# VectorE's exp banks chosen while scores are ordered, other spare banks in the first block, and PV of the last units ahead of other work

**The chip, the cores and the metric.** One core of one Trainium2 chip. The metric is the device time of one execution. It is the span of the trace plus about 1.83 us.

## The reference, cut to what matters

```python
xn = _layernorm(x)                          # x: 1 x 2048 x 448, bf16
s = _A_ref(xn, A_wqkv, A_wo)                # 16 heads of 28: softmax(q k^T / sqrt(28)) v, then @ wo
g = _silu(_B_ref(xn, w1, b1, w2, b2))       # gelu MLP, 448 -> 1792 -> 448
return x + s * g
```

The exponential (exp) of 16 x 2048 x 2048 scores is the main work. PV below is the product of these probabilities with v, on TensorE (PE).

## The kernel before

The program is written by a scheduler on the host. Processes yield tasks with a modelled duration; the scheduler always takes the task with the earliest modelled start, and appends it to the list of its engine. On the chip each engine has its list and waits on semaphores; that PE keeps to the order of its list shows below, in a stand of 1.65 us with the next scores queued behind it. The modelled durations therefore fix the order.

```python
def start_of(self, t):                      # the model's earliest start of a task
    s = self.tE[t.E]
    for b in t.reads:
        ...
        s = max(s, b.tw + SEM)              # SEM = 0.07 us after the modelled write
    ...
```

A block is one group of four heads by 512 queries: 64 score banks (128x512 f32 each). Block 0 works in units of two banks, the others in units of three; a ring of six banks holds two units. The third bank of some units (from a table, `LATE`) is exponentiated by VectorE with a polynomial, in pairs; ScalarE exponentiates the rest.

```python
COUNTS = (5, 4, 5, 4, 5, 5, 5, 6, 1, 6, 6, 6, 6, 4)     # VectorE's banks per block 1..14
...
    _b0 = 2 * (_i % 2) if _i < 32 else 3 * (_i % 2)     # first ring bank of a unit
...
K.banks += [(K.ring[:, b, :], K.b_ring[b]) for b in (5, 4)]   # block 0's spares
```

`p_busy` adds filler matmuls where the model sees PE under 85% busy; they are meant to keep PE's clock up. (In the first trace of before the granted clock was 1.00 from 7.57 to 475.20 us and 0.50 after, and PE had been busy 1.98 of the 3.41 us before the fall.)

## Time and profile before

| | before |
|---|---|
| time, median of 3 | 487.23 us |
| span of the traced run (its time was 488.98 us) | 487.2 us |
| first exp starts | 13.50 us |
| first exp to the end of the last | 464.84 us |
| after the last exp | 8.83 us |
| ScalarE / VectorE / PE busy | 96% / 84% / 93% |

The lines of the profile are in the prediction.

### The profile page before, as it was taken

What the parts mean: (1) busy time and instruction counts of PE and PEld (TensorE: products, weight loads), DVE (VectorE), ACT (ScalarE), POOL (GpSimd) and SP (SyncE); (2) the same over time, 40 slices, a digit from 0 to 9 for tenths busy, and PEclk for the clock granted to TensorE, in tenths of its full rate; (3) what the DMA queues carried; (4) which work ended last, traced back from release to release, by engine and by line L of the source; (5) the groups of instructions that cost most, each with busy time, mean ns of one, the idle gap of its engine ahead of it and who ended that gap; (6) DMA issues with size and microseconds to landing.
All of it is one profiled execution on the core that took longest, in us unless ns stands there. A gap on an engine that the chain in (4) does not pass through costs nothing.

```text
span 487.2 us, 9867 instructions
## 1 busy us (share of the span) xinstructions
PE 451.6 (93%) x4107; PEld 174.2 (36%) x4107; DVE 407.6 (84%) x566; ACT 469.5 (96%) x391; POOL 85.4 (18%) x91
## 2 busy tenths in 40 slices
PE   6999999999999999999999999999999999999875
PEld 4443333333233333232333343333233443343432
DVE  8745998779996998998999499899898989999553
ACT  4999999999999999999999999999999999999992
POOL 6472112031021113020111041110200202020100
PEclk9999999999999999999999999999999999999995
DMA  8401000000000000000400000000100010001210
GB/s 251 142 12 25 1 0 1 1 1 1 2 1 1 0 1 1 1 2 1 133 1 0 1 1 1 1 2 1 38 1 2 1 39 0 1 20 60 90 44 20
DMA packets 8286, 11.07 MB, mean 23 GB/s; under 512 B 1649, under 2 KB 6897, under 8 KB 8242
## 3 DMA queue, kind: packets, MB, share of 16 engines
q1 hardware_dynamic: 8098, 10.21, 6.9%
q8 instruction: 32, 0.52, 0.4%
q10 hardware_dynamic: 144, 0.23, 0.1%
q14 instruction: 12, 0.10, 0.1%
HBM read 8.61 MB, written 1.84 MB: 21 GB/s over the span
## 4 chain that ended last, share of the span: by engine, by line
ACT 43%; PE 29%; issue 17%; DVE 9%; POOL 1%; ACTq 0%; DVEq 0%
ACT P L1115 38%; PE ring L1086 8%; PE acc L1234 5%; PE misc L1034 4%; ACT h L1013 3%; PE misc L692 2%; PE acc L823 2%; PE misc L976 2%; DVE x_sb L1142 1%; PE misc L1323 1%; PE acc L805 1%; DVE x_sb L1193 1%; DVE kT L1187 1%; PE ring L976 1%; POOL rlo L1299 1%
## 5 line engine op out<-in xcount | busy, mean ns | idle before, releaser
L1115 ACT ACTIVATE P<-ring 128x1536 bf16<-128x1536 f32 (+1 forms) x350 | 428.8, 1461 | 2.6 <-PE ring L1086 2.0
L1086 PE MATMUL ring<-qT,kT 32*128 32x512 bf16 (+1 forms) x1208 | 136.3, 350 | 20.7 <-ACT P L1115 16.4
L1234 PE MATMUL acc<-P,vaug 128*32 128x512 bf16 (+1 forms) x1140 | 96.2, 354 | 0.1
L1086 PEld LDWEIGHTS ring<-qT,kT 32*128 32x128 bf16 x1208 | 36.7, 91 | 125.9 <-ACT P L1115 113.2
L1298 POOL CAST rhi<-rc 128x512 bf16<-128x512 f32 x15 | 18.1, 1206 | 228.5 <-DVE rc L1294 185.5
L1142 DVE TENSOR_SCALAR x_sb<-ring 128x512 int32<-128x512 f32 x68 | 46.7, 686 | 9.4 <-PE ring L1086 8.6
L1034 PE MATMUL misc<-w,h 128*128 128x448 bf16 x224 | 52.3, 355 | 0.0
L823 PE MATMUL acc<-ident,zero 128*128 128x128 bf16 x588 | 49.9, 221 | 0.0
L1234 PEld LDWEIGHTS acc<-P,vaug 128*32 128x32 bf16 x1140 | 26.0, 95 | 53.7 <-issue 48.0
L899 POOL TENSOR_TENSOR qsq<-qT 128x512 bf16<-128x512 bf16 x15 | 21.8, 1454 | 129.6 <-DVE qT L894 123.2
L823 PEld LDWEIGHTS acc<-ident,zero 128*128 128x128 bf16 x588 | 33.7, 98 | 22.5 <-issue 21.1
L976 PE MATMUL misc<-xnT,w 128*128 128x512 bf16 x140 | 38.5, 382 | 0.1
L1193 DVE SCALAR_TENSOR_TENSOR x_sb<-x_sb,kT 128x1024 uint16<-128x1024 int32 (+1 forms) x22 | 28.2, 1280 | 0.3
L1191 DVE SCALAR_TENSOR_TENSOR kT<-kT 128x1024 f32<-128x1024 f32 (+1 forms) x22 | 27.6, 1252 | 0.3
L959 DVE CAST h<-misc 128x512 bf16<-128x512 f32 x35 | 24.0, 687 | 4.4 <-PE misc L976 3.8
L1187 DVE SCALAR_TENSOR_TENSOR kT<-kT 128x1024 f32<-128x1024 f32 (+1 forms) x22 | 27.2, 1238 | 0.4
L1189 DVE SCALAR_TENSOR_TENSOR kT<-kT 128x1024 f32<-128x1024 f32 (+1 forms) x22 | 26.5, 1203 | 0.3
L1034 PEld LDWEIGHTS misc<-w,h 128*128 128x128 bf16 x224 | 17.3, 97 | 22.7 <-issue 11.8
L1299 POOL TENSOR_TENSOR rlo<-rc,rhi 128x512 bf16<-128x512 f32 x15 | 22.3, 1489 | 1.2
L1187 DVE SCALAR_TENSOR_TENSOR w<-w 128x1024 f32<-128x1024 f32 (+1 forms) x19 | 21.8, 1149 | 0.3
L1193 DVE SCALAR_TENSOR_TENSOR x_sb<-x_sb,w 128x1024 uint16<-128x1024 int32 (+1 forms) x19 | 21.2, 1114 | 0.1
L1189 DVE SCALAR_TENSOR_TENSOR w<-w 128x1024 f32<-128x1024 f32 (+1 forms) x19 | 20.8, 1094 | 0.2
(144 smaller groups left out, 479.2 us busy)
## 6 DMA issues: line engine op xcount, KB each, us to landing
h<-in_A_x_dram SPq DMA_DIRECT2D x4, 448.0 KB, 3.5
w<-in_B_w_dram SPq DMA_DIRECT2D x1, 1568.0 KB, 7.2
x_sb<-in_A_x_dram SPq DMA_DIRECT2D x3, 448.0 KB, 6.0
w<-in_B_w_dram SPq DMA_DIRECT2D x1, 1344.0 KB, 8.2
out_dram<-h SPq DMA_DIRECT2D x6, 224.0 KB, 2.4
h<-in_A_wqkv_dram SPq DMA_DIRECT2D x3, 168.0 KB, 5.5
out_dram<-h SPq DMA_DIRECT2D x4, 112.0 KB, 1.7
wo<-in_A_wo_dram SPq DMA_DIRECT2D x16, 24.5 KB
```

Source lines behind the costliest of these rows:

```text
L823: ins = eng.matmul(K.acc[:, 0:128], K.zero[:, :], K.ident[:, :], start=False, stop=True, skip_group_check=True)
L976: ins = eng.matmul(bank, K.w1[:, kt, ft * 128:(ft + 1) * 128], K.xnT[:, kt, c * 512:(c + 1) * 512], start=(kt == 0), stop=(kt == KT - 1))
L1034: ins = eng.matmul(ps, hv[:, ft, t * 128:(t + 1) * 128], K.w2[:, ft, :], start=(ft == 0), stop=(ft == FT - 1))
L1086: return eng.matmul(K.ring[:, RB[m], col:col + nq], K.kT[32 * j:32 * j + 32, g, t * 128:(t + 1) * 128], K.qT[32 * j:32 * j + 32, g, c * 51 ...
L1115: return eng.activation(K.P[:, p0:p0 + n, :], K.ring[:, b0:b0 + n, :], ACTF.Exp, scale=SM_SCALE)
L1142: yield _Task(DVE, lambda eng, m=m, i=i, half=half: eng.tensor_scalar(K.ysb[i][:, 512 * half:512 * half + 512], K.ring[:, RB[m], :], SM_SC ...
L1187: yield _Task(DVE, lambda eng: eng.scalar_tensor_tensor(u, v, EXP_A, v, op0=ALU.add, op1=ALU.mult), [tv], [tu], d1, 0.0, 4)
L1189: yield _Task(DVE, lambda eng: eng.scalar_tensor_tensor(u, u, EXP_B, u, op0=ALU.add, op1=ALU.mult), [tu], [tu], d1, 0.0, 4)
L1191: yield _Task(DVE, lambda eng: eng.scalar_tensor_tensor(u, v, EXP_D, u, op0=ALU.mult, op1=ALU.add), [tv, tu], [tu], d1, 0.0, 4)
L1193: yield _Task(DVE, lambda eng: eng.scalar_tensor_tensor(pl.bitcast(dt.uint16), y, 2.0 ** -9, u, op0=ALU.mult, op1=ALU.add), ty + [tu], [K. ...
L1234: return eng.matmul(K.acc[32 * j:32 * j + 32, q0:q0 + nq], K.vaug[:, t, 4 * g + j, :], ap[:, col:col + nq], tile_position=(0, 32 * j), sta ...
L1299: yield _Task(En, lambda eng: eng.tensor_tensor(K.rlo[:, :, :], rcb, K.rhi[:, :, :], ALU.subtract), [K.b_rc, K.b_rhl], [K.b_rhl], d2, 0.0, 1)
```

## The change

The intent: let the scheduler give a bank to VectorE when VectorE's modelled backlog allows it, remove a wait where block 0's two-bank units meet the first three-bank unit, and shorten the end. The core of the diff (cut):

```diff
-LATE, PAIR = set(), {}
...
-COUNTS = (5, 4, 5, 4, 5, 5, 5, 6, 1, 6, 6, 6, 6, 4)
...
+    UBASE.append(4 * (_u % 2) if _u < 32 else 3 * (_u % 2))
...
+LATE_GAP, LATE_TH, LATE_SLACK, LATE_SUB = 3, 8.0, 6.0, 14
...
-        K.banks += [... for b in (5, 4)]
+        K.banks += [... for b in (3, 2)]
...
 def pe_low(self):
-        return ... < HAM_LOW * HAM_WIN
+        return ... < (HAM_LOW if K.exp_u < NU - 20 else 1.1) * HAM_WIN
 def p_busy(self):
-        while K.exp_u < NU - 1:
+        while K.exp_u < NU - 2:
...
 def p_silu(self, c):                       # VectorE's multiplies
-                        ... 0.63, 0.0, 6)
+                        ... 0.63, 0.0, 3)
 def p_scores(self):
+            K.assign(u)                    # chooses ScalarE's and VectorE's banks of unit u
-            ... + 0.02 * (len(fl) - len(ms))
+            ... + 0.005 * (len(fl) - len(ms))
+    def pick_late(self, u):
+        ...
+        left = (n - 1 - r) / 3.0 * 1.364 + LATE_SLACK
+        if K.open:
+            if u - K.open.u < LATE_GAP:
+                return False
+            if K.backlog() + 3.6 > left:
+                K.close()
+                return False
+            ...                            # the second bank of the open pair
+        else:
+            bl = K.backlog()
+            ...
+            if not K.ys or bl > LATE_TH or bl + 4.8 > left or sub > LATE_SUB:
+                return False
+            ...                            # opens a pair, takes one of two buffers
 def p_pv(self):
-                        lambda: 1.2 if K.exp_u - K.pv_u > 4 or GU - 1 <= K.exp_u <= GU else 6)
+                        lambda: 1.2 if K.exp_u - K.pv_u > 4 or K.exp_u > NU - 4 or GU - 1 <= K.exp_u <= GU else 6)
```

In `p_pv` the modelled duration of block 15's PV is shortened too; that edit is not shown, and below "the edit of `p_pv`" means the rank line alone.

More of the change, by code (lines that the diff above doesn't have):

```diff
@@ L29 @@
 MTOT = NBLK * T * 4
-LATE, PAIR = set(), {}
-OFFS = {0: (), 1: ((7,),), 2: ((0,), (7,)), 3: ((0, 3), (10,)), 4: ((0, 3), (7, 11)), 5: ((0, 3), (6, 9), (13,)),
-        6: ((0, 3), (6, 9), (11, 13)), 7: ((0, 2), (4, 7), (9, 11), (13,)), 8: ((0, 2), (4, 6), (8, 10), (12, 14)),
-        9: ((0, 1), (3, 5), (6, 8), (10, 12), (14,))}
-COUNTS = (5, 4, 5, 4, 5, 5, 5, 6, 1, 6, 6, 6, 6, 4)
 GM = 64 * 9 + 6
 MPAIRS = [tuple(64 * 9 + x for x in p) for p in ((16, 21), (26, 31), (36, 41), (46, 51))]
-for _ms in MPAIRS:
-    LATE.update(_ms)
-    for _m in _ms:
-        PAIR[_m] = _ms
@@ L42 @@
-MLATE = set(LATE)
-_seq = [m for m in range(64, MTOT) if m not in MLATE]
-_US = [list(range(m, m + 2)) for m in range(0, 64, 2)] + [_seq[i:i + UB] for i in range(0, len(_seq), UB)]
-GU = min(u for u, ms in enumerate(_US) if ms[-1] >= GM)
-for _b in range(1, NBLK - 1):
-    _th = [ms[2] for ms in _US if len(ms) == 3 and ms[2] // 64 == _b and ms[2] % 64 >= 4]
-    for _o in OFFS[COUNTS[_b - 1]]:
-        _ms = tuple(_th[x] for x in _o)
-        LATE.update(_ms)
-        for _k in _ms:
-            PAIR[_k] = _ms
@@ L54 @@
-UNITS, RB, PB, RPREV, PPREV, UOF = [], {}, {}, {}, {}, {}
-_last, _plast, _p = {}, {}, 0
-for _i, _ms in enumerate(_US):
-    _b0 = 2 * (_i % 2) if _i < 32 else 3 * (_i % 2)
-    _na = len([m for m in _ms if m not in LATE])
-    if _p + _na > NP:
-        _p = 0
-    UNITS.append((_ms, _ms[:_na], _b0, _p))
-    for _k, m in enumerate(_ms):
-        UOF[m] = len(UNITS) - 1
-        RB[m] = _b0 + _k
-        RPREV[m] = _last.get(RB[m])
-        _last[RB[m]] = m
-        if _k < _na:
-            PB[m] = _p + _k
-            PPREV[m] = _plast.get(PB[m])
-            _plast[PB[m]] = m
-    _p += _na
+MLATE = set(m for ms in MPAIRS for m in ms)
@@ new lines @@
+_seq = [m for m in range(64, MTOT) if m not in MLATE]
+UNITS = [list(range(m, m + 2)) for m in range(0, 64, 2)] + [_seq[i:i + UB] for i in range(0, len(_seq), UB)]
+GU = min(u for u, ms in enumerate(UNITS) if ms[-1] >= GM)
+RB, RPREV, UOF, UBASE, _last = {}, {}, {}, [], {}
+for _u, _ms in enumerate(UNITS):
+    UBASE.append(4 * (_u % 2) if _u < 32 else 3 * (_u % 2))
+    for _k, _m in enumerate(_ms):
+        UOF[_m] = _u
+        RB[_m] = UBASE[_u] + _k
+        RPREV[_m] = _last.get(RB[_m])
+        _last[RB[_m]] = _m
@@ L97, in __init__ @@
         self.tr = 0.0
+class _Pair:
+    __slots__ = ("i", "u", "ms", "done", "closed")
+    def __init__(self, i, u, m):
+        self.i, self.u, self.ms, self.done, self.closed = i, u, [m], 0, False
 class _Task:
@@ L414, in schedule @@
         K.pv_done = [False] * MTOT
-        K.late_left = [len([m for m in LATE if m // 64 == b]) for b in range(NBLK)]
+        K.late = set(MLATE)
+        K.late_left = [len([m for m in MLATE if K.sub_of(m) == b]) for b in range(NBLK + 3)]
+        K.late_q = deque()
+        K.late_on = False
+        K.open = None
+        K.dve_q = 0.0
+        K.PB, K.PPREV, K.plast, K.pptr = {}, {}, {}, 0
+        K.act_ms, K.p0 = [None] * NU, [0] * NU
         K.ys, K.pls, K.pl_use = [0, 1], [0, 1, 2], [0, 0, 0]
@@ L418, in schedule @@
         K.late_blk = 0
-        K.banks += [(K.ring[:, b, :], K.b_ring[b]) for b in (5, 4)]
+        K.banks += [(K.ring[:, b, :], K.b_ring[b]) for b in (3, 2)]
         K.outs = []
@@ L429, in schedule @@
         K.spawn(K.p_scores(), 0)
-        K.spawn(K.p_take(4), 0)
-        K.spawn(K.p_take(5), 0)
+        K.spawn(K.p_take(2), 0)
+        K.spawn(K.p_take(3), 0)
         K.spawn(K.p_exps(), 0)
@@ L757, in tr @@
         def tr(pr, h):
-            bank, tok = ring(2 * h + pr)
+            bank, tok = ring(4 * h + pr)
             psb = bank.bitcast(dt.bfloat16)
@@ L771, in trev @@
             for h in range(2):
-                bank, tok = ring(2 * h + pr)
+                bank, tok = ring(4 * h + pr)
                 src = bank.bitcast(dt.bfloat16)[:, 0:512].rearrange("p (k n) -> p k n", k=2)
@@ L813, in pe_low @@
             K.pe_hist.popleft()
-        return sum(b - max(a, now - HAM_WIN) for a, b in K.pe_hist) < HAM_LOW * HAM_WIN
+        return sum(b - max(a, now - HAM_WIN) for a, b in K.pe_hist) < (HAM_LOW if K.exp_u < NU - 20 else 1.1) * HAM_WIN
     def p_busy(self):
@@ L825, in f @@
             return ins
-        while K.exp_u < NU - 1:
-            yield ("until", lambda: K.pe_low() or K.exp_u >= NU - 1)
+        n = 0
+        while K.exp_u < NU - 2:
+            yield ("until", lambda: K.pe_low() or K.exp_u >= NU - 2)
             yield _Task(PE, f, [K.b_id, K.b_pads], [K.b_acc], DUM, 0.1, 95)
+            n += 1
+            if n > 2000:
+                raise RuntimeError("stuck")
     def p_k0(self):
@@ L982, in p_direct @@
         K = self
-        s0 = UNITS[GU - 1][2]
+        s0 = UBASE[GU - 1]
         for i, (c, f0) in enumerate(DIRECT):
@@ L995, in p_gelu @@
         left = [FT] * C
-        s0 = UNITS[GU - 1][2]
+        s0 = UBASE[GU - 1]
         for q, pc in enumerate(PIECES):
@@ L1052, in p_silu @@
                                                                        op0=ALU.add, op1=ALU.mult),
-                        [K.b_sig[c % 2], K.b_fsb[c % 2]], [K.b_h[c], K.b_g[c]], 0.63, 0.0, 6)
+                        [K.b_sig[c % 2], K.b_fsb[c % 2]], [K.b_h[c], K.b_g[c]], 0.63, 0.0, 3)
         K.g_done[c] = True
@@ L1074, in p_scores @@
         for u in range(NU):
-            ms = UNITS[u][0]
+            ms = UNITS[u]
             fl, rd = [], []
@@ L1103, in p_scores @@
             yield ("until", lambda: all(RPREV[m] is None or K.ring_rel[RPREV[m]] for m in ms))
-            yield _Task(PE, fall, rd, [K.b_ring[RB[m]] for m in ms], 0.17 + 0.05 * len(ms) + 0.02 * (len(fl) - len(ms)), 0.1, 1)
+            K.assign(u)
+            yield _Task(PE, fall, rd, [K.b_ring[RB[m]] for m in ms], 0.17 + 0.05 * len(ms) + 0.005 * (len(fl) - len(ms)), 0.1, 1)
             K.sc_u = u
@@ L1109, in p_exps @@
         for u in range(NU):
-            _, ms, b0, p0 = UNITS[u]
+            yield ("until", lambda: K.sc_u >= u)
+            ms, b0, p0 = K.act_ms[u], UBASE[u], K.p0[u]
             n = len(ms)
-            yield ("until", lambda: K.sc_u >= u and all(PPREV[m] is None or K.pv_done[PPREV[m]] for m in ms))
+            yield ("until", lambda: all(K.PPREV[m] is None or K.pv_done[K.PPREV[m]] for m in ms))
             def fexp(eng, b0=b0, p0=p0, n=n):
@@ L1120, in p_exps @@
             K.exp_u = u
-            K.exp_m = UNITS[u + 1][0][0] - 1 if u + 1 < NU else MTOT - 1
+            K.exp_m = UNITS[u + 1][0] - 1 if u + 1 < NU else MTOT - 1
             if u >= NU - 2:
@@ L1131, in p_late @@
                 b.r += x.r
-        for u in range(NU):
-            for m in UNITS[u][0]:
-                if m not in LATE:
-                    continue
-                half = PAIR[m].index(m)
-                if half == 0:
-                    yield ("until", lambda: K.sc_u >= u and len(K.ys) > 0)
-                    i = K.ys.pop(0)
-                else:
-                    yield ("until", lambda: K.sc_u >= u)
-                yield _Task(DVE, lambda eng, m=m, i=i, half=half: eng.tensor_scalar(
-                    K.ysb[i][:, 512 * half:512 * half + 512], K.ring[:, RB[m], :], SM_SCALE * LOG2E * 65536.0,
-                    127.0 * 65536.0, op0=ALU.mult, op1=ALU.add),
-                            [K.b_ring[RB[m]]], [K.b_y[i][half]], 0.69, 0.0, 1)
-                K.ring_rel[m] = True
-                if m == PAIR[m][-1]:
-                    K.spawn(K.p_exp2(PAIR[m], i), m)
+        K.late_on = True
@@ new lines, in p_late @@
+        while K.sc_u < NU - 1 or K.late_q:
+            yield ("until", lambda: K.sc_u == NU - 1 or (K.late_q and UOF[K.late_q[0][0]] <= K.sc_u))
+            if not K.late_q:
+                return
+            m, i, half, pair = K.late_q.popleft()
+            yield _Task(DVE, lambda eng, m=m, i=i, half=half: eng.tensor_scalar(
+                K.ysb[i][:, 512 * half:512 * half + 512], K.ring[:, RB[m], :], SM_SCALE * LOG2E * 65536.0,
+                127.0 * 65536.0, op0=ALU.mult, op1=ALU.add),
+                        [K.b_ring[RB[m]]], [K.b_y[i][half]], 0.69, 0.0, 1)
+            K.dve_q -= 0.69
+            K.ring_rel[m] = True
+            pair.done += 1
+            if pair.closed and pair.done == len(pair.ms):
+                K.spawn(K.p_exp2(tuple(pair.ms), i), m)
@@ new lines, in backlog, with close @@
+    def backlog(self):
+        K = self
+        t = max(0.0, K.tE[DVE] - K.now) + K.dve_q
+        for p in K.procs:
+            if isinstance(p[3], _Task) and p[3].E == DVE and p[3].prio != 4 and p[3].prio != 1:
+                st = K.start_of(p[3])
+                if st is not None and st < K.now + 1.0:
+                    t += p[3].dur
+        return t
+    def close(self):
+        K = self
+        p, K.open = K.open, None
+        p.closed = True
+        if p.done == len(p.ms):
+            K.spawn(K.p_exp2(tuple(p.ms), p.i), p.ms[-1])
@@ new lines, in pick_late @@
+    def pick_late(self, u):
+        K = self
+        ms = UNITS[u]
+        m = ms[-1]
+        sub = K.sub_of(m)
+        if K.open and (u - K.open.u > LATE_GAP + 2 or K.sub_of(K.open.ms[0]) != sub):
+            K.close()
+        n = 64 if sub < NBLK - 1 else 16
+        r = m % n
+        if len(ms) < 3 or not K.late_on or sub == 0 or r < 4 or GU - 1 <= u <= GU + 1:
+            return False
[4 more added lines that the diff above has]
+            if K.backlog() + 3.6 > left:
+                K.close()
+                return False
+            p = K.open
+            p.ms.append(m)
+            K.late_q.append((m, p.i, 1, p))
+            K.close()
+        else:
+            bl = K.backlog()
+            one = max(bl, 4.1) + 7.2 > left
+            if not K.ys or bl > LATE_TH or bl + 4.8 > left or sub > LATE_SUB:
+                return False
+            p = _Pair(K.ys.pop(0), u, m)
+            K.late_q.append((m, p.i, 0, p))
+            K.open = p
+            if one:
+                K.close()
+        K.late.add(m)
+        K.late_left[sub] += 1
+        K.dve_q += 3.6
+        return True
@@ L1150, in p_mlate, with assign @@
+    def assign(self, u):
+        K = self
+        ms = UNITS[u][:-1] if K.pick_late(u) else UNITS[u]
+        if K.pptr + len(ms) > NP:
+            K.pptr = 0
+        for k, m in enumerate(ms):
+            K.PB[m] = K.pptr + k
+            K.PPREV[m] = K.plast.get(K.pptr + k)
+            K.plast[K.pptr + k] = m
+        K.act_ms[u], K.p0[u] = ms, K.pptr
+        K.pptr += len(ms)
     def p_mlate(self):
@@ L1155, in p_mlate @@
             i = K.ys.pop(0)
+            K.dve_q += 7.2
             for half, m in enumerate(ms):
@@ L1166, in p_mlate @@
                     127.0 * 65536.0, op0=ALU.mult, op1=ALU.add), [tok], [K.b_y[i][half]], 0.69, 0.0, 1)
+                K.dve_q -= 0.69
                 K.banks.append((bank, tok))
@@ L1195, in p_exp2 @@
                     ty + [tu], [K.b_pl[k]], d1, 0.0, 4)
+        K.dve_q -= 2.91 * len(ms)
         K.ln2e = 0
@@ L1209, in p_pv @@
             first, end = K.sub_of(ms[0]), K.pieces(ms[-1])[3]
-            b = q // 16
+            b = first
             yield ("until", lambda: K.exp_m >= ms[-1] and K.E_done >= first - 1 and (
-                not end or len([x for x in K.late_ready if x[0] // 64 == b]) == K.late_left[b]))
+                not end or len([x for x in K.late_ready if K.sub_of(x[0]) == b]) == K.late_left[b]))
             late = []
             for m, k, half in list(K.late_ready):
-                hole = (4 * q + m % 4) in LATE and all(m % 4 != x[0] % 4 for x in late)
-                if m // 64 == b and (end or (K.ready([K.b_pl[k]]) and (hole or len(K.late_ready) - len(late) > 3))):
+                hole = (4 * q + m % 4) in K.late and all(m % 4 != x[0] % 4 for x in late)
+                if K.sub_of(m) == b and (end or (K.ready([K.b_pl[k]]) and (hole or len(K.late_ready) - len(late) > 3))):
                     late.append((m, k, half))
@@ L1220, in p_pv @@
             K.late_left[b] -= len(late)
-            src = [(m, K.P[:, PB[m], :], K.b_P[PB[m]]) for m in ms if m not in LATE]
+            src = [(m, K.P[:, K.PB[m], :], K.b_P[K.PB[m]]) for m in ms if m not in K.late]
             src += [(m, K.plate[k][:, 512 * half:512 * half + 512], K.b_pl[k]) for m, k, half in late]
@@ L1227, in p_pv @@
                     _, j, pc, _, s = K.pieces(m)
-                    g = b // C
+                    g = q // 16 // C
                     if kk >= len(pc):
@@ L1244, in fall @@
                 return ins
-            yield _Task(PE, fall, rd, [K.b_acc], 0.36 if len(fl) < 5 else 0.6, 0.1,
-                        lambda: 1.2 if K.exp_u - K.pv_u > 4 or GU - 1 <= K.exp_u <= GU else 6)
+            yield _Task(PE, fall, rd, [K.b_acc], 0.36 if len(src) < 5 else 0.6, 0.1,
+                        lambda: 1.2 if K.exp_u - K.pv_u > 4 or K.exp_u > NU - 4 or GU - 1 <= K.exp_u <= GU else 6)
             for m in ms:
```

## The prediction

Passages that told of the hardware what no trace or run of this case shows are cut from the text below, and the cuts are marked. None of them is a term of its sum, which came to 482.5 us. The 0.1 to 0.2 us for a semaphore in part 3 compare with 0.15 us in tail_only's trace, from the end of the last exp (478.26) to the PV that waits for it (478.41).

> **What bounds the kernel now.** I read the page first (busy shares, slices), then the groups by form, the waits, the table of stretches, the end of the chain of waits, and the timeline of the switch out of block 0.
>
> ```profile
> PE 451.6 (93%) x4107; PEld 174.2 (36%) x4107; DVE 407.6 (84%) x566; ACT 469.5 (96%) x391; POOL 85.4 (18%) x91
> PEclk9999999999999999999999999999999999999995
> ...
> L1115 ACT ACTIVATE P<-ring 128x1536 bf16<-128x1536 f32 x249 | 350.6, 1602 | 1.2 <-PE ring L1086 0.9
> L1115 ACT ACTIVATE P<-ring 128x1024 bf16<-128x1024 f32 x100 | 108.9, 1119 | 1.4 <-PE ring L1086 1.1
> L1142 DVE TENSOR_SCALAR x_sb<-ring 128x512 int32<-128x512 f32 x68 | 46.7, 686 | 9.4 <-PE ring L1086 8.6
> ...
> ACT P L1115 <- PE ring L1086: 2.0, 4, 0.7
> ...
> 13.50:45.80 32.30, 31.33 (x285) 13.40 (x284) 17.63 (x37) 30.66 (x37) 15.93 (x20) 1.00 0.19 56
> 45.80:449.30 403.50, 383.41 (x3184) 141.22 (x3183) 360.39 (x456) 402.87 (x317) 57.89 (x41) 1.00 0.03 9
> 449.30:478.30 29.00, 23.80 (x530) 12.15 (x531) 14.85 (x30) 29.00 (x23) 2.20 (x2) 0.95 0.21 65
> 478.30:487.20 8.90, 3.81 (x54) 1.56 (x44) 3.39 (x7) 0.04 (x1) 0.00 (x0) 0.50 0.08 26
> ```
>
> In the last four lines the columns are PE, PEld, DVE, ACT, POOL, then the granted clock. The stretches are block 0, blocks 1 to 14, block 15 and the tail after the last exp. ScalarE is busy 402.87 of 403.50 us in blocks 1 to 14: exp on ScalarE is the bound there, and only exp taken off ScalarE shortens them. PE's 93% is no second bound: 588 of its matmuls are fillers (line 823, 49.9 us busy)[...]. Outside the exps there are three fixed pieces: 13.5 us before the first exp, 27 us of gelu in block 9, and 8.9 us after the last exp.
>
> The kernel computes 1024 score banks (128x512). VectorE makes 76 of the exponentials (68 here, 8 during gelu) with a five-instruction polynomial; ScalarE makes 948, in 350 instructions of mostly three banks. Read from the starts of the exp instructions, a three-bank exp follows its predecessor by 1.33 us and a two-bank one by 0.904 us, so a bank moved to VectorE saves ScalarE 1.33 - 0.904 = 0.426 us. (The mean durations 1602 and 1119 overlap their neighbours and must not be used for this.)
>
> The tail and the switch out of block 0:
>
> ```profile
> 477.60 0.48 PE misc L1323
> 478.08 0.97 PE acc L1234 x32
> 479.05 1.23 PE ring L1323 x3
> 480.29 0.55 PE acc L1234 x16
> 480.83 0.45 PE acc L823 x3
> ...
> 481.30 0.30 DVE E_sb L1266
> ...
> 44.92 0.33 PE L823 MATMUL acc<-ident,zero 128*128 128x128 bf16 x3
> 45.32 0.61 PE L1086 MATMUL ring<-qT,kT 32*128 32x512 bf16 x6
> 45.75 1.45 ACT L1115 ACTIVATE P<-ring 128x1536 bf16<-128x1536 f32 x1 [0.58 <-PE ring L1086]
> ```
>
> The last exp ends at 478.34. PE, at half clock since about 475.3 (granted 0.60 in 475 to 476, 0.50 after), does older PV (x32), then an output projection (line 1323, 1.23 us), then the PV that the end needs (x16), then a filler. Only at 481.30 can VectorE read the accumulator: 2.96 us after the last exp.
>
> [...]the trace's scalar-tensor-tensor groups have means of 1227 to 1314 ns. [...]Here the clock fell although PE was busy 1.08 of 2.00 us in 472 to 474[...]. [...]the four last output transfers land after a median 1.7 us, and this part does not change.
>
> **The change part by part.**
>
> 1. Choice of VectorE's banks. The fixed table (68 banks) goes; when a unit of scores is ordered, its third bank is given to VectorE if the modelled backlog is under 8 us, a buffer is free and the work fits before the block's end. Units stay as they are, so the exp count stays 350; each added bank turns a three-bank exp into a two-bank one. How many can VectorE take? A bank costs 0.686 (eviction) plus half a pair: about (0.78 + 4 x 1.26)/2 = 2.91, together 3.6 us. In blocks 1 to 14 VectorE is busy 360.4 us; less 76 x 3.6 = 274 leaves 87 us of other work. Its fullest blocks (3, 11, 12, 13) still show 1.9 to 2.3 us idle each, as short gaps between instructions; I take 1.9 of a 27 us block as unavoidable, about 28 us of the 403.5. Usable: 403.5 - 28 - 87 = 288 us, or 80 banks, against 76. By block, idle above 1.9 us is 4.0 in block 2, 2.4 in block 4, about 5 in block 9 (twice as long, so twice the allowance), 3 elsewhere: 14.6 us, also 4 banks. So the table was already near VectorE's limit. I expect 4 more, 72 for 68, with a spread of -2 to +8: 4 x 0.426 = 1.7 us, all of it on the path.
>
> 2. Spare banks in block 0. Before, block 0's pairs use ring banks 0,1 and 2,3 and the spares are 4,5; the first three-bank unit (0,1,2) must wait for the exp that reads 2,3. That is the last line above: 0.58 us idle, 0.75 us start to start (1.655 instead of 0.904). With pairs on 0,1 and 4,5 it finds bank 2 free. Gain 0.75 us; nothing else in block 0 changes its order of need.
>
> 3. PV of the last units first, and fillers. In the last 20 units fillers take every modelled PE hole, so the clock should not fall near 475. At full clock the second-last exp is not late: it starts 1.73 us before the last one instead of 1.33, so 0.4 us. PV of the last units outranks the output projection from the fourth-last unit on, so PE has nothing old to do when the last exp ends: semaphore 0.1 to 0.2, PV x16 0.41 (its duration at 461 to 468), and no filler behind it. The accumulator is read about 0.7 us after the last exp, not 2.96: 2.2 us less. Then the same ladder, 481.30 to 485.03, with one or two matmuls at full clock: 0.2 less. Against this: the projection that needs only three groups (x3, 0.74 at full clock) may still be placed just ahead of the last PV because it can start earlier, 0.4 back. Sum 0.4 + 2.2 + 0.2 - 0.4 = 2.4 us.
>
> 4. Silu's multiplies on VectorE go ahead of the polynomial, and modelled durations of block 15's scores and PV are shortened to what the trace has (0.40 us per 12 score matmuls). ScalarE waits for nothing in block 15 until its last unit, so 0 us; I allow 0.2 us of loss for more two-bank units, whose short exps leave PE less time for the next scores.
>
> Sum: 487.2 - 1.7 - 0.75 - 2.4 + 0.2 = 482.5 us.
>
> **The rivals.** (a) VectorE is the real limit, and the dynamic choice yields no more banks, or fewer, since it also refuses near block ends and makes some lone banks (0.686 + 3.17 = 3.85 us). For: fullest blocks at 91 to 93%. Against: blocks 2, 4 and 9 have room. Then only parts 2 and 3 remain: about 484. (b) A fuller VectorE queue delays what others wait for: evictions hold ring banks, the accumulator copy at a block's end comes late, PV falls behind, and ScalarE waits for P banks. For: an eviction sits behind instructions of 1.2 us or more. Against: in blocks 1 to 14 ScalarE waits almost not at all, and 21 P banks are seven units, about 9 us of slack. That would eat 1 to 3 us: 484 to 486. (c) The tail hardly shortens: the clock still falls, or fillers and the early projection stand before the last PV. For: the PE queue is in order. Then 1.5 us less gain: 484. (d) VectorE fills its holes almost completely, 8 more banks, and the tail gains 2.9: about 480.
>
> **Range and chances.** The terms are independent enough: banks 0 to 3.4 us, switch 0.4 to 0.8, tail 1 to 3, losses 0 to 2. I put 8 in 10 between 479.0 and 486.0. Faster by over 2% needs less than 477.5, that is 9.7 us; (d) does not get there, so 0.05. Slower by over 2% needs a broken overlap in all blocks: 0.02. Within 2%: 0.93.
>
> **What would show it.** Right: evictions from the ring at 70 to 76, two-bank exps up and three-bank ones down by the same number, 350 in all; no wait of ScalarE at the switch out of block 0; granted clock 1.00 until the last exp; about 1 us from the last exp's end to the accumulator copy; after it some 3.5 us of VectorE and PE ladder and 2 us of output transfer. Wrong: fewer evictions than 68 (part 1), ScalarE idle above 1 us in blocks 1 to 14 (part 4 and rival b), a clock of 0.5 at the last PV or a projection before it (part 3). What would make the whole wrong is a new wait of ScalarE on PE or on P banks in every block.

## More of the kernel before

At a block's end, VectorE copies the accumulator, GpSimd spreads the reciprocals of the sums (`rhi`, `rlo`), and PE transposes them:

```python
def p_epi(self, b):
    ...
    En, d1, d2 = POOL, 0.62, 1.05                       # modelled GpSimd durations
    yield _Task(En, ... tensor_copy(K.rhi, rcb) ..., d1, 0.0, 1)
    yield _Task(En, ... tensor_tensor(K.rlo, rcb, K.rhi, ALU.subtract) ..., d2, 0.0, 1)
    bank2, tok2 = yield ("bank", lambda: K.ready([K.b_rhl], 0.2))
    ...                                                 # eight small matmuls on PE: rhi, rlo
```

## The result, and the profile after

The median is 490.41 us (489.85 to 490.57, 4 runs) against 487.23 us: slower by 0.64% (ratio 1.0064, 95% interval 1.0047 to 1.0082), and outside the predicted range, though within the 2% that the prediction gave 0.93. A ratio is the mean time of one kernel's fast runs over that of the other's of the same rounds, so not quite the ratio of the medians.

The same views of the changed kernel: the page, the groups by form, the waits of ScalarE, and the stretches (block 0, blocks 1 to 14, block 15, tail; columns as before).

```profile
PE 449.2 (92%) x4143; PEld 177.4 (36%) x4179; DVE 404.8 (83%) x580; ACT 470.7 (96%) x391; POOL 86.5 (18%) x91
...
L1109 ACT ACTIVATE P<-ring 128x1536 bf16<-128x1536 f32 x250 | 348.8, 1559 | 2.8 <-PE ring L1078 2.6
L1109 ACT ACTIVATE P<-ring 128x1024 bf16<-128x1024 f32 x99 | 104.7, 1098 | 2.0 <-PE ring L1078 1.1 <-PE acc L1295 0.3
L1132 DVE TENSOR_SCALAR x_sb<-ring 128x512 int32<-128x512 f32 x67 | 45.9, 686 | 10.4 <-PE ring L1078 9.5
...
ACT P L1109 <- PE ring L1078: 3.7, 5, 1.2
...
13.70:45.30 31.60, 30.07 (x276) 13.06 (x279) 16.99 (x36) 30.50 (x37) 15.97 (x20) 1.00 0.20 62
45.30:453.30 408.00, 380.68 (x3150) 140.96 (x3179) 359.81 (x473) 404.51 (x318) 59.55 (x41) 1.00 0.04 12
453.30:482.20 28.90, 27.92 (x636) 16.97 (x634) 13.82 (x27) 28.88 (x23) 1.66 (x2) 1.00 0.08 27
482.20:488.50 6.30, 1.22 (x20) 0.42 (x18) 2.99 (x7) 0.00 (x0) 0.00 (x0) 0.80 0.11 36
```

Read: 67 banks for VectorE, not more than 68 but one less; blocks 1 to 14 took 408.0 us instead of 403.5; ScalarE was idle 3.5 us there instead of 0.6; the tail is 6.3 us instead of 8.9 of the first trace.

To find waits that "busy" hides, compare the ends of successive exps. In every trace here a three-bank exp that waits for nothing ends 1.343 us after its predecessor's end, a two-bank one 0.917 us, and whatever is above that is a wait. (The prediction used starts. Recorded starts of exps that queue up creep ahead of the ends, 1.330 against 1.343 us, so gaps between starts overstate waits.) In us, from the two traces:

| part | before | after | difference | predicted |
|---|---|---|---|---|
| exps, if none waited (948 and 949 banks) | 426.60 | 427.02 | +0.43 | -1.7 |
| waits inside block 0, with two short layer-norm stretches | 2.23 | 2.23 | 0 | 0 |
| wait at the switch out of block 0 | 0.69 | 0 | -0.69 | -0.75 |
| other waits in blocks 1 to 14 | 1.03 | 4.87 | +3.84 | +0.2 |
| waits in block 15 | 0.01 | 0.01 | 0 | -0.4 |
| tail, in these two traces | 8.83 | 6.32 | -2.51 | -2.0 |

Gelu and the four tanh are the same in both (34.19 and 34.20 us). Three rows carry the error: the exps, the waits, and the tail, whose 8.83 us turns out not to be typical.

The largest wait is one place, in block 14. The timeline there, changed kernel (start, duration, engine, line, and in brackets the idle time before it and who ended it):

```profile
433.07 1.50 POOL L1359 CAST rhi<-rc 128x512 bf16<-128x512 f32 x1 [22.23 <-DVE rc L1355]
...
434.42 0.39 PE L1078 MATMUL ring<-qT,kT 32*128 32x512 bf16 x3 [0.35 <-ACT P L1109]
434.62 1.21 DVE L1251 SCALAR_TENSOR_TENSOR kT<-kT 128x1024 f32<-128x1024 f32 x1
434.65 2.09 POOL L1360 TENSOR_TENSOR rlo<-rc,rhi 128x512 bf16<-128x512 f32 x1
...
436.79 0.23 PE L1369 MATMUL misc<-ident,rhi 128*128 128x128 bf16 x1 [1.65 <-POOL rlo L1360]
...
437.35 0.39 PE L1078 MATMUL ring<-qT,kT 32*128 32x512 bf16 x3
...
437.78 2.79 ACT L1109 ACTIVATE P<-ring 128x1536 bf16<-128x1536 f32 x2 [1.15 <-PE ring L1078]
...
440.79 0.61 PE L1078 MATMUL ring<-qT,kT 32*128 32x512 bf16 x3
...
441.44 3.98 ACT L1109 ACTIVATE P<-ring 128x1536 bf16<-128x1536 f32 x3 [0.87 <-PE ring L1078]
```

PE stands 1.65 us in front of an epilogue transpose that needs GpSimd's `rlo`; the next scores are queued behind it, and ScalarE runs dry (1.15 us). Then a second wait of 0.87 us follows, with scores of 0.61 us instead of 0.39. The stretches show why (columns as above, the clock is the third number from the right):

```profile
434.00:436.00 2.00, 0.79 (x9) 0.20 (x7) 1.83 (x3) 2.00 (x3) 1.92 (x2) 1.00 0.00 0
...
438.00:439.00 1.00, 1.00 (x11) 0.41 (x9) 1.00 (x2) 1.00 (x1) 0.00 (x0) 0.57 0.00 0
439.00:441.00 2.00, 2.00 (x10) 0.71 (x8) 0.38 (x2) 1.57 (x2) 0.00 (x0) 0.50 0.00 0
```

PE, busy 0.79 of 2.00 us in 434 to 436 and 1.21 in 436 to 438, lost its clock: granted 0.50 from 438.14 to 441.56. (In hold13, below, PE does not stand there, was busy 1.92 and 1.86 us in the same stretches, and its clock stayed at 1.00.) By ends of exps, the two waits are 1.26 and 0.98 us.

GpSimd was planned at 0.62 + 1.05 us and took 1.50 + 2.09 us. Its instructions in the changed kernel (duration in ns: least/median/most):

```profile
L1359 POOL CAST rhi<-rc x15: 611/1477/1499, 49.5 to 458.7; 128x512 bf16<-128x512 f32 x15
L1360 POOL TENSOR_TENSOR rlo<-rc,rhi x15: 1046/1049/2089, 50.2 to 459.4; 128x512 bf16<-128x512 f32 x15
```

The planned values are the least ones. The long ones lie beside VectorE's polynomial (its SCALAR_TENSOR_TENSOR instructions, which read two tensors): it ran at 432.92 and 434.62, and GpSimd's 2.09 us is 1.04 over its least. Each of the four `rlo` of 1.90 us and more began while such an instruction ran, and the pair that no VectorE instruction overlaps (458.66 and 459.35) took 0.61 and 1.05 us. VectorE's are longer there too: of the 1024-element f32 polynomial instructions of the changed kernel, 61 that overlap no GpSimd instruction took 1217 ns on average, and 32 that overlap one took 1372, up to 1951. (No run takes GpSimd's instructions away, so this cause of its slowness rests on the overlap alone, and what the two engines contend for is not shown; that PE's stand behind it costs the time is tested below.) The old kernel had the same spread (`rlo` 1047 to 2089 ns), so it is no news of the change; what is new is where in PE's order it hits.

### The profile page after: what moved, and what is told of

It is laid out like the page before. It is cut to its first block, busy times and chain, and to the rows that moved or that the text cites. A ratio compares the mean times of both kernels' runs of the same rounds, so it can differ in the third digit from the quotient of the medians.

```text
span 488.5 us, 9994 instructions
## 1 busy us (share of the span) xinstructions
PE 449.2 (92%) x4143; PEld 177.4 (36%) x4179; DVE 404.8 (83%) x580; ACT 470.7 (96%) x391; POOL 86.5 (18%) x91
## 4 chain that ended last, share of the span: by engine, by line
PE 37%; ACT 29%; issue 18%; DVE 12%; POOL 2%; DMA 1%; ACTq 0%; DVEq 0%; POOLq 0%
ACT P L1109 24%; PE ring L1078 11%; PE acc L1295 7%; PE misc L1026 5%; PE acc L811 4%; ACT h L1005 3%; PE misc L968 3%; PE misc L680 2%; DVE x_sb L1253 2%; PE misc L1384 1%; POOL rlo L1360 1%; DVE x_sb L1132 1%; ACT w L1040 1%; DVE st L615 1%; DVE kT L1247 1%
## 5 line engine op out<-in xcount | busy, mean ns | idle before, releaser
L1295 PE MATMUL acc<-P,vaug 128*32 128x512 bf16 (+1 forms) x1141 | 93.8, 351 | 2.1 <-DVE E_sb L1345 0.7
L1359 POOL CAST rhi<-rc 128x512 bf16<-128x512 f32 x15 | 19.5, 1297 | 239.7 <-DVE rc L1355 198.3
L811 PE MATMUL acc<-ident,zero 128*128 128x128 bf16 x660 | 56.4, 221 | 1.1 <-POOL qsq L891 0.6
L811 PEld LDWEIGHTS acc<-ident,zero 128*128 128x128 bf16 x660 | 38.6, 98 | 24.5 <-issue 20.5
L891 POOL TENSOR_TENSOR qsq<-qT 128x512 bf16<-128x512 bf16 x15 | 23.7, 1581 | 122.6 <-DVE qT L886 100.8
L1295 PEld LDWEIGHTS acc<-P,vaug 128*32 128x32 bf16 x1141 | 24.5, 94 | 49.6 <-issue 42.3
L968 PE MATMUL misc<-xnT,w 128*128 128x512 bf16 x127 | 36.7, 382 | 2.0 <-issue 1.5
L1251 DVE SCALAR_TENSOR_TENSOR kT<-kT 128x1024 f32<-128x1024 f32 (+1 forms) x23 | 25.8, 1121 | 0.3
L1253 DVE SCALAR_TENSOR_TENSOR x_sb<-x_sb,kT 128x1024 uint16<-128x1024 int32 (+1 forms) x23 | 25.5, 1110 | 0.3
L1247 DVE SCALAR_TENSOR_TENSOR kT<-kT 128x1024 f32<-128x1024 f32 (+1 forms) x23 | 25.5, 1107 | 0.3
L1249 DVE SCALAR_TENSOR_TENSOR kT<-kT 128x1024 f32<-128x1024 f32 (+1 forms) x23 | 25.1, 1092 | 0.3
L1251 DVE SCALAR_TENSOR_TENSOR w<-w 128x1024 f32<-128x1024 f32 (+1 forms) x21 | 23.2, 1105 | 0.2
L1247 DVE SCALAR_TENSOR_TENSOR w<-w 128x1024 f32<-128x1024 f32 (+1 forms) x21 | 22.7, 1079 | 0.3
L1249 DVE SCALAR_TENSOR_TENSOR w<-w 128x1024 f32<-128x1024 f32 (+1 forms) x21 | 22.7, 1082 | 0.1
```

The costliest lines, as they stand in the source:

```text
L811: ins = eng.matmul(K.acc[:, 0:128], K.zero[:, :], K.ident[:, :], start=False, stop=True, skip_group_check=True)
L968: ins = eng.matmul(bank, K.w1[:, kt, ft * 128:(ft + 1) * 128], K.xnT[:, kt, c * 512:(c + 1) * 512], start=(kt == 0), stop=(kt == KT - 1))
L1247: yield _Task(DVE, lambda eng: eng.scalar_tensor_tensor(u, v, EXP_A, v, op0=ALU.add, op1=ALU.mult), [tv], [tu], d1, 0.0, 4)
L1249: yield _Task(DVE, lambda eng: eng.scalar_tensor_tensor(u, u, EXP_B, u, op0=ALU.add, op1=ALU.mult), [tu], [tu], d1, 0.0, 4)
L1251: yield _Task(DVE, lambda eng: eng.scalar_tensor_tensor(u, v, EXP_D, u, op0=ALU.mult, op1=ALU.add), [tv, tu], [tu], d1, 0.0, 4)
L1253: yield _Task(DVE, lambda eng: eng.scalar_tensor_tensor(pl.bitcast(dt.uint16), y, 2.0 ** -9, u, op0=ALU.mult, op1=ALU.add), ty + [tu], [K. ...
```

## The experiments

Twelve runs. The changed kernel again, two parts of it alone, and one cure.

**after_again**, unedited.

> The changed kernel once more, as the control for the three runs beside it. From the two traces: the last exp ends 3.84 us later than before (482.18 against 478.34) and the tail after it is 2.5 us shorter (6.3 against 8.8). Expected: 489 to 490.5 us, ratio to the kernel before 1.003 to 1.007, and again ScalarE waits of more than 1 us near 436 us.

Measured: 490.19 us (489.50 to 490.41), ratio 1.0042 (1.0026 to 1.0059). As expected; first exp to last 468.39 us (468.44 in the first trace), again a wait near 436 us, here 1.76 us by ends, with the clock down from about 437 to 440 (mean of the run 0.993). What was not expected are the 11 runs of the kernel before: spans of 484.9 to 485.5 us with a mean clock of 0.996 to 0.999 (4 runs) and 486.2 to 487.2 with 0.988 to 0.989 (7). My trace of before was one of the second kind, and the median of 487.23 us was of the first (487.23 - 1.83 = 485.4).

**tail_only**: before, with the edits of `pe_low`, `p_busy` and `p_pv` of the diff above.

> The kernel before with two parts of the change alone: fillers in every modelled PE hole over the last 20 units, stopped one unit earlier, and PV of the last units first. Banks, block 0 and the table of VectorE's banks as before. Theory 1 (the tail gain is real and independent of the choice of banks): last exp 0.4 us earlier because the clock holds, tail 2.5 us shorter, so 487.2 - 2.9 = 484.3 us, granted clock 1.00 until the last exp. Rival (the shorter tail in the changed kernel comes with the later last exp, as older work was done before it): within 0.7 us of 487.2.

Measured: 486.97 us (486.39 to 488.91), ratio 0.9988 (0.9966 to 1.0009): not told from before, and theory 1's 484.3 us is refuted. (Its four spans with the clock up, 484.6 to 485.2 us, lie 0.3 us below those of before, 484.9 to 485.5.) In its trace the accumulator is copied 0.6 us after the last exp, as predicted, and the tail is 6.33 us. But first exp to last is 464.85 us, as before: the 0.4 us of the last unit was never lost. And two of six runs still had a mean clock of 0.989 and a span of 487.1.

**late_only**: the changed kernel with all other parts taken back (banks, fillers, `p_pv`, durations, silu's rank).

> The kernel before with the dynamic choice of VectorE's banks alone; spare banks, fillers and the tail as before. It chooses 68 banks from the ring, as many as the old table, so the count costs nothing. Theory 1 (the loss is new ScalarE waits, from the order that the choice brings to PE's and VectorE's queues): 489 to 491.5 us, ScalarE waits in blocks 1 to 14 up by 2 to 4 us over the 3.2 us of before. Rival (the loss in the changed kernel is the missing banks and the other parts): 487.2, within 0.7 us.

Measured: 489.87 us (489.78 to 490.14), ratio 1.0037 (1.0020 to 1.0055); first exp to last 467.82 us, 2.97 more than before with the same 68 banks. So the loss comes without a missing bank: 1.3 us more waits in blocks 1 to 14, 0.8 in the stretch with gelu, and 0.85 in block 15, where the clock was down from 457 to 464 (mean of the run 0.992). One of these waits again has PE 1.19 us in front of an epilogue transpose for `rlo`, at 414 us, another block than in the changed kernel.

**hold13**: one line of the changed kernel.

```diff
-        bank2, tok2 = yield ("bank", lambda: K.ready([K.b_rhl], 0.2))
+        bank2, tok2 = yield ("bank", lambda: K.ready([K.b_rhl], -2.4 if b == 13 else 0.2))
```

> The changed kernel with one edit: PE's eight small transposes of block 13's epilogue (they need GpSimd's rhi and rlo) are put into PE's order no earlier than 2.4 us after the modelled end of GpSimd's work instead of up to 0.2 us before it. The order is the same up to 434 us, and the same banks are chosen. Theory 1 (PE, in order, stands behind GpSimd for 1.65 us, ScalarE runs out of scores, and the idle PE then loses its clock for 3 us, a second wait of ScalarE): 2.34 us of waits (1357 + 984 ns) go, so 2.0 to 2.4 us less than after_again. Rival (VectorE's backlog holds the ring banks or P banks there, or the longer block 14 is due to work that must be done anyway): less than 0.5 us.

Measured: 487.56 us (487.47 to 488.14), 2.6 us less than the changed kernel beside it (490.19); first exp to last 465.92, 2.5 us less. Theory 1 holds. The same place in its trace:

```profile
434.31 2.09 POOL L1360 TENSOR_TENSOR rlo<-rc,rhi 128x512 bf16<-128x512 f32 x1
...
435.01 0.39 PE L1078 MATMUL ring<-qT,kT 32*128 32x512 bf16 x3
...
436.43 0.39 PE L1078 MATMUL ring<-qT,kT 32*128 32x512 bf16 x3
436.76 0.23 PE L1369 MATMUL misc<-ident,rhi 128*128 128x128 bf16 x1
```

GpSimd is as slow as ever (2.09 us), but two units of scores now stand ahead of the transposes; PE does not wait, ScalarE does not, and the clock was 1.00 there.

The tail's two parts apart, a general cure, and more banks.

**pv_only**: before, with the edit of `p_pv` alone.

> The kernel before with one part of the tail change alone: PV of the last units first. The earlier runs showed that the kernel before has two kinds of run: with mean clock 0.996 to 0.999 its span is 484.9 to 485.5, with 0.988 to 0.989 it is 486.2 to 487.2; my trace of before was of the second kind. Theory 1 (what the tail change saves is mostly what a falling clock costs, and PV first is worth a few tenths when the clock holds): shortest spans 484.3 to 484.8, and the runs with the low clock still occur, at 486 or less since the needed PV no longer stands behind half-speed projections. Rival (PV first is worth the 2.2 us that I predicted): all spans at most 484.5.

Measured: 487.82 us (486.29 to 488.07), ratio 0.9975 (0.9953 to 0.9997). Two runs had a clock of 1.000 (spans 484.4 and 484.6), four 0.992 to 0.994 (485.7 to 486.3); before in this call: three at 485.1 to 485.4, eight at 486.2 to 488.0 (0.984 to 0.989). That is theory 1: a few tenths when the clock holds, more when it falls, and the falling goes on.

**fillers_only**: before, with the edits of `pe_low` and `p_busy` alone.

> The kernel before with the other part of the tail change alone: fillers in every modelled PE hole in the last 20 units, stopped one unit earlier. Theory 1 (fillers keep the clock up to the last exp): the kind of run with mean clock 0.988 to 0.989 vanishes or nearly so, spans 484.9 to 485.5. Rival ([...]fillers that the scheduler places in modelled holes do not change it): that kind stays as frequent as in the kernel before, 7 of 11 runs, with spans of 486.2 to 487.2.

Measured: 487.22 us (486.63 to 489.02), ratio 0.9982 (0.9959 to 1.0005): four runs at 484.8 to 485.4, two still at 487.2 with 0.988. Between theory and rival: too few runs to say that fillers make the fall rarer, enough to say that they do not prevent it.

**margin05**: the changed kernel, PE's background work planned later.

```diff
-            s = max(s, b.tw + SEM)
+            s = max(s, b.tw + (SEM if t.E != PE or not (t.prio > 1 and self.exp_u < NU - 14) else 0.5))
```

> The changed kernel with one edit in its scheduler: every PE task but the scores, up to the last 14 units, is planned no earlier than 0.5 us after the modelled end of what it reads (0.07 before), so that PE's order leaves room for GpSimd and VectorE being later than modelled. Same number of banks (67 from the ring). Theory 1 (the loss is PE, in order, standing behind late results with scores queued after): ScalarE waits in blocks 1 to 14 fall from 7.2 us to 3 to 4.5 us, so 2.5 to 4 us less than the changed kernel: 486 to 487.5 us. Rival (only the one wait in block 14 mattered and the rest is the price of two-bank units): within 0.7 us of the run with block 13's epilogue held, 487.6 us. If VectorE's load is the cause: no better than the changed kernel, 490 us.

Measured: 488.47 us (488.25 to 488.66), 1.9 us less than the changed kernel's first median (490.41) and 0.9 more than hold13. They were run at other times. Waits in blocks 1 to 14 by ends are 2.93 us, down from 4.87. The direction is theory 1's, the size only the rival's: a margin of 0.5 us is less than the 1.9 us by which GpSimd was late, and it drew a new order with new waits (PE 0.86 us in front of a transpose at 142 us, this one released by VectorE).

**gap1**: the changed kernel with `LATE_GAP` 1 instead of 3, which makes it choose 73 banks.

> The changed kernel with the least distance between the two banks of a pair 1 unit instead of 3: the choice then takes 73 banks from the ring instead of 67. By ScalarE's price of 0.426 us a bank that is 2.6 us less exp. Theory 1 (VectorE is full: with two buffers in flight it has no room, and more banks come back as waits): waits of ScalarE grow by more than 2.6 us, total 490 to 494 us. Rival (my prediction's step: VectorE had room for more banks, and the rule left it unused): 487 to 488.5 us.

Measured: 492.10 us (491.59 to 492.40), ratio 1.0072 (1.0050 to 1.0094). Six banks fewer on ScalarE are 2.55 us less exp, yet first exp to last is 469.44 us, 1.0 more: the waits grew by 3.6 us (one of 2.64 at 434 us, one of 1.59 at 187 us). More banks by this rule do not pay.

A second trace of before, the remaining part alone, one more cure, and a version to beat both.

**before_again**, unedited, one look.

> The kernel before, unedited, for a second trace of it. If it falls in the kind of run whose mean clock is 0.996 or more (4 of 11 and 3 of 11 runs so far), then theory (most of the 8.8 us tail in my first trace was the fallen clock) expects the tail after the last exp at 7.0 to 7.3 us and no 0.4 us wait before the last unit; the rival (the order of the last PV alone made it 8.8 us) expects 8.5 to 9 us. If it falls in the other kind, it repeats the first trace.

Measured: span 486.3 us, clock 0.989 (one run, so its state is unknown; both numbers are those of the second kind of run), and neither case as I had put them. The clock fell twice, once from 455 to 461 us (granted 0.51 in 455 to 462), which cost ScalarE 0.99 us in block 15, and again after 482. At the last exp it was up. The last exp ended at 479.52. The end of its chain of waits, then that of the changed kernel, whose last exp ended at 482.18:

```profile
479.08 0.74 PE ring L1323 x3
479.82 0.34 PE acc L1234 x16
480.16 0.29 PE acc L823 x3
480.45 0.02 issue
480.47 0.30 DVE E_sb L1266
...
482.50 0.57 PE ring L1323
```

```profile
481.75 0.74 PE ring L1384 x3
482.49 0.37 PE acc L1295 x16
482.86 0.02 issue
482.88 0.30 DVE E_sb L1327
...
484.91 0.38 PE ring L1384
```

Old order, the clock up at the last exp: 0.95 us from the last exp to the copy, and a tail of 6.77 us. New order: 0.70 and 6.32 us. But of these 0.45 us, 0.20 are not the order's: here the clock fell at 482.34, just before the last projection, which took 0.57 us instead of 0.38. The trace of fillers_only, with the old order and the clock up until 483.69, has 0.95 and 6.58 us. So the reordering is worth 0.25 us, not 2.4: the filler behind the last PV is gone, while the projection (x3, 0.74 us) still stands before that PV in both orders. The other 2.25 us of the first trace's 8.83 (less 6.58) were half clock (granted 0.50 after 475.20); in pv_only's trace (mean clock 0.994), at half clock when the last exp ends, the new order has 1.58 us to the copy where the first trace has 2.96.

**banks_only**: before, with ring banks 0,1 and 4,5 for block 0's units and 2,3 as spares.

```diff
-    _b0 = 2 * (_i % 2) if _i < 32 else 3 * (_i % 2)
+    _b0 = 4 * (_i % 2) if _i < 32 else 3 * (_i % 2)
-        K.banks += [(K.ring[:, b, :], K.b_ring[b]) for b in (5, 4)]
+        K.banks += [(K.ring[:, b, :], K.b_ring[b]) for b in (3, 2)]
```

> The kernel before with the change of block 0's banks alone. Theory 1 (the switch out of block 0 costs 0.75 us and its removal is a plain gain): the wait at the switch goes, span 0.75 us shorter than before. Rival (the order of all later work is chained to it: with the old table and silu's low rank, the scheduler then plans 20 us of background work after the last exp, where it planned 5): the wait goes, but the tail after the last exp is 18 to 24 us and the time 500 to 506 us.

Measured: 501.87 us (501.79 to 502.17), ratio 1.0293 (1.0272 to 1.0313). The rival holds. The wait at the switch is gone, but the stretch after the last exp is

```profile
478.20:500.10 21.90, 12.82 (x102) 5.84 (x100) 18.20 (x38) 1.70 (x1) 0.00 (x0) 0.83 0.25 84
```

21.9 us long: 38 VectorE instructions of silu and of the output that used to lie under the exps. "Removing a wait in block 0" re-drew the order of everything after it.

**hold_pv**: hold13 and one more.

```diff
+            if end and (b in (4, 6, 7)):
+                yield ("until", lambda: K.ready([K.b_pl[x[1]] for x in K.late_ready if K.sub_of(x[0]) == b], -1.0))
```

> The run hold13 with one further edit: at the ends of blocks 4, 6 and 7 the last PV is planned no earlier than 1.0 us after VectorE's last probabilities are modelled as done. In hold13 PE stands 1.07 us behind a VectorE instruction that takes 1.41 us instead of 0.69 while GpSimd works, and ScalarE waits 0.90 us; at 211 and 237 us it waits 0.36, 0.45 and 0.32. Theory 1 (those waits too are PE standing behind late VectorE results with scores queued after): the 0.9 goes and some of the other 1.1 us, 0.9 to 1.6 us less than hold13. Rival (two-bank units leave PE too little time at a block's end whatever the order): under 0.4 us less.

Measured: 487.37 us (486.92 to 487.62); first exp to last 465.37, 0.55 us less than hold13, between the two ranges. First hold13, then hold_pv at the end of block 4:

```profile
154.32 1.42 POOL L891 TENSOR_TENSOR qsq<-qT 128x512 bf16<-128x512 bf16 x1 [16.70 <-PE acc L811]
...
154.88 1.41 DVE L1253 SCALAR_TENSOR_TENSOR x_sb<-x_sb,w 128x512 uint16<-128x512 int32 x1
...
156.34 0.40 PE L1295 MATMUL acc<-P,vaug 128*32 128x512 bf16 x4 [0.57 <-DVE x_sb L1253]
```

```profile
155.00 1.41 DVE L1253 SCALAR_TENSOR_TENSOR x_sb<-x_sb,w 128x512 uint16<-128x512 int32 x1
...
156.25 0.39 PE L1078 MATMUL ring<-qT,kT 32*128 32x512 bf16 x3 [0.19 <-ACT P L1109]
...
157.18 0.40 PE L1297 MATMUL acc<-P,vaug 128*32 128x512 bf16 x4
```

VectorE's instruction takes 1.41 us in both (0.69 alone); with scores ahead of the PV that needs it, PE no longer stands there. The wait was 0.66 us by ends (my 0.90 was by starts); others shrank or moved.

**table_hold**: before with its table, block 0's new banks, the edits of `pe_low`, `p_busy`, `p_pv` and of the modelled durations, silu's old rank, and

```diff
-        bank2, tok2 = yield ("bank", lambda: K.ready([K.b_rhl], 0.2))
+        bank2, tok2 = yield ("bank", lambda: K.ready([K.b_rhl], -3.2 if b > 0 else 0.2))
```

> A version meant to beat both: the old table of VectorE's banks (68), block 0's new banks, fillers and PV first at the end, the shortened modelled durations, silu's old rank, and in every block after the first PE's epilogue transposes planned 3.2 us later than before. From the traces: exp portion of before 464.85 us, less 0.75 (switch), 0.4 (last unit) and 0.5 (the wait on GpSimd at 188 us), and a tail of 6.3 us after a start of 13.4 to 14.0: spans of 483.0 to 484.0, times of 484.8 to 485.8 us, ratio 0.993 to 0.996. If the order of later work changes as in the run with block 0's banks alone, it can be slower than before instead.

Measured: 485.78 us (485.38 to 486.14, 6 runs), ratio 0.9961 (0.9945 to 0.9978). All six spans, 483.6 to 484.3, are below every span of before (484.8 and up). First exp to last is 463.83 us: the switch is gone, and other waits in blocks 1 to 14 are 0.70 us instead of 1.03. It beats both kernels, and it keeps the table.

## Why the prediction was wrong, point by point

**Part 1, VectorE's banks: failed.** "I expect 4 more, 72 for 68" gave 67. The capacity sum (80 banks) took all of VectorE's idle time above 28 us as usable at any time. The rule cannot use it so: printed while the program was built, of its refusals 123 came with both buffers in flight and the modelled backlog above 8 us at once (70 of these also too near the block's end) and 70 from the least distance in a pair; the backlog alone refused once, the buffers alone never, so these counts do not tell which of the two holds the choice back. A buffer is held from the choice to the end of the polynomial; the choice takes four banks in the first ten units of a block, then waits, and takes one more: five in nearly every block, where the table gave 4 to 6. The value of a bank, 0.426 us, was right (1.343 - 0.917). The term was +0.43 instead of -1.7, and gap1, which did take 73, was slower still.

**Part 2, the switch: right in size, wrong in one clause.** 0.69 us by ends for 0.75. "Nothing else in block 0 changes its order of need" may be so, but everything after it changes, as banks_only shows.

**Part 3, the tail: the end point right, the saving not.** The accumulator is read 0.70 us after the last exp (predicted 0.7), although the projection still stands before the last PV, which the prediction had allowed for. But "2.96 us" was read from a run of 488.98 us whose clock had fallen, and set against a median of 487.23 us. In a trace of before with the clock up it is 0.95. The term is about 0.25, not 2.4; the "0.4 us" of the last unit was a gap between recorded starts, 0.01 by ends. And "the clock should not fall" does not follow from fillers: it still fell in two of six runs of tail_only and of fillers_only.

**Part 4, waits: the step that decided.** "I allow 0.2 us of loss" became 3.84 us. Rival (b) named the right kind, late results that others wait for, and even 1 to 3 us, but it looked at evictions, P banks and the accumulator copy, and not at PE's own order. PE worked through its matmuls in the program's order, as the 1.65 us stand shows: the scores queued behind it began only at 437.35, and in hold13, with two units of scores ahead of the transposes, there is no stand. The views before the prediction had the lines that warn: "PEld misc" waiting for `rlo` (1.8 us in 4 waits) was among the waits of before, and GpSimd's mean durations (1206 and 1489 ns) stood far above the modelled 0.62 and 1.05.

**Sum.** With the measured terms: +0.43 - 0.69 + 3.84, less about 0.25 of tail, is +3.3 us, against 3.18 between the medians. Of the 7.9 us between 482.5 and 490.41, the waits are 3.6, the tail 2.15 and the banks 2.1. hold13 shows that 2.5 us of the waits are one place. late_only shows that the new choice, with an equal count, brings such waits by itself. What stays open: the 1.3 us of waits that remain in hold13 above before (0.8 in hold_pv) are many of 0.1 to 0.4 us behind two-bank units and at block ends; I have not shown whether the front-loaded choice or the new order as such makes them. (table_hold has block 0's new banks, the fillers, PV first and the shortened durations without such waits, but also a hold of the transposes in every block.) Nor is it settled what makes PE's clock fall in some runs of one kernel and not in others. The traces give a lead that no run tests: in all 14, every change of the granted clock lies a whole multiple of 3.41 us after the first rise to full clock (before: 137 steps from 7.57 to 475.20 us; the changed kernel: 126 and 127 from 8.06 to 438.14 and 441.56), and where this grid lies against the program differs from run to run. In before_again PE was busy 2.49 us of the step 451.62 to 455.03 and the clock fell at its end; in the first trace of before the grid lay 0.16 us earlier against the first exp, PE was busy 2.60 us of the step 451.30 to 454.71, and it did not fall there. A plain threshold of PE's busy share does not fit: late_only kept its clock after a step with 1.81 of 3.41 us.

## What to carry to other kernels

An order fixed ahead by a model is only as good as the model's worst duration, not its best: put work that waits on an engine with uneven durations (here `rlo`, 1046 to 2089 ns) behind the work that feeds the bottleneck engine, in the queue that both share (hold13: 2.6 us less). A small gain early in such a schedule re-draws everything after it (banks_only: the wait of 0.69 us gone, the time 14.6 us longer), so test each part in place, and compare parts by the trace as well as by the total. Check that the traced run is one of the runs whose time is quoted.

## Measured on the way

- Exps in a row on ScalarE end 1.343 us apart for 1536 elements and 0.917 for 1024, so 0.426 us per 512 elements; a straight line through the two leaves 0.065 us that does not depend on the length (an estimate from these two numbers).
- Recorded starts of queued exps creep ahead of their ends (1.330 against 1.343 us apart, durations growing from 1816 to 1949 ns over eleven exps of the first trace of before), so a gap of 0.40 us between starts before the last exp was 0.01 us between ends.
- PE's clock fell without PE being fully idle: the changed kernel's at 438.14 us, after PE was busy 0.79 of 2.00 us and 1.21 of the next 2.00. The spans of the kernel before lie between 484.8 us (mean clock 0.996 to 0.999) and 488.0 us (0.984).
- Where GpSimd and VectorE overlap, a GpSimd instruction of 1.05 us is recorded with up to 2.09 us, and a 512-element VectorE one of 0.69 with 1.41: numbers for planning.
